# Re-weighting and interleaving the background feed of an FFT-convolution plus feed-forward kernel

## The chip, the cores and the metric

The kernel runs on one core of one Trainium2 chip. TensorE (PE) does the matmuls, VectorE (DVE) and ScalarE (ACT) the elementwise work, GpSimd (POOL) some elementwise work and one DMA queue, SyncE (SP) the other DMA queue. The metric is the device time of one execution in microseconds; a time is given as the median of its runs.

## The reference

Two stages are computed, in fp32. The first is a long convolution: `u = x * v` is convolved along the sequence (12480 positions, 4 batches, 128 channels) with a filter that a small network makes from position embeddings, and the result is multiplied by `x`. The second sends all 49920 tokens through a gated feed-forward layer of width 2048.

```python
h_filt = (np.maximum(pos_emb @ w1, 0.0) @ w2) * np.exp(-0.01 * pos)[:, None]
Uf = np.fft.rfft(x * v, n=2 * S, axis=1)
Hf = np.fft.rfft(h_filt, n=2 * S, axis=0)
y = np.fft.irfft(Uf * Hf[None, :, :], n=2 * S, axis=1)[:, :S, :]
a = (x * y).reshape(B * S, D)
h = a @ w_in
out = (h * (1.0 / (1.0 + np.exp(-1.702 * h)))) @ w_out
```

## The kernel before

**The work.** The sequence is cut in two blocks and the four batches are taken in parts, which gives five sets, numbered 0 to 4 (`SETS`). For each set the convolution has three phases. First transforms (`p1_unit`, 26 a set) multiply `x` and `v`, fold the product, split it in two parts (`uh` on ACT at L295, `ul` on DVE at L298) and do a first Fourier stage on PE (L178 to L180), storing to DRAM `g_d`. Spectral units (`p2_unit`, 31 a set) load `g_d`, do the second stage forward on PE (L324), multiply spectra on DVE, do the inverse on PE (L330, copied out at L473) and store `z_d`. Output units (`p3_unit`, 104 in all) load `z_d` on POOL's queue (L499), do the last inverse stage on PE (L520) and multiply by `x`, which gives the input tiles `xh` and `xl` of the feed-forward layer.

**Set 3 and 4 differ from 1 and 2 in their spectral units.** They belong to the second block and also add the product of the older spectrum: on DVE two products at L419 or L423, the products with the forward's result at L438 and L439, the adds at L441 and L443, and the final subtract and add that give `y` at L463 and L464. A spectral unit of set 1 or 2 has its products at L459 and L461 instead.

**The feed-forward steps.** `Ffn.mm1` (L592 to L594) and `Ffn.mm2` (L609) run 832 times, eight for each output unit; one such pair is called a step here, t = 0 to 831. A step's matmuls of the second layer come three steps behind those of the first. Between them DVE makes `fgl` (L600) from two ACT results, `fgh` and `fg`; `fg` has two buffers.

**The order.** It is written out by hand. Set 0's first two phases run ahead of the steps. From step `HOLD` on, each step gives sets 1 to 4 a share of the background work by `feed.run(1.0)`; at every eighth step an output unit of the current set is started (`p3.tick`). At step `HOLD` a pool is closed, its memory taken over and the padding of `z_d` filled with zeros. The output units of sets 1 to 4 begin at steps 95, 199, 407 and 615; a set's spectral units have to be done by then, and `feed.reach` gives out what is left.

**The planner.** `conv_feed` lists the units in order, each with a weight, and a mark (the sum of weights) for the end of each set's spectral units. `Feed.pace` sets the rate so that a mark is reached in a given number of steps. Starting a unit lets every unit that is still in `Pipe` go on to its next `yield` (a tick); a `yield 1` within a tick ends an atom only. `Feed.run` gives out the n-th atom of a tick when the goal passes `base + w * n / size`, where `size` is the number of atoms of the tick before; atoms beyond that number fall due at `base + w`. Units of `None` start nothing and only move the pipe on. A first transform takes seven ticks (loads, constants, small network, product and fold, `ul`, matmuls, store), a spectral unit of set 3 or 4 six (loads, nothing, forward with all DVE work, nothing, inverse registered, store). The inverse of a unit is issued ahead of the next unit's forward (`behind`) or at its own last tick.

**Buffers that matter.** `ft`, the constants of a first transform, has four buffers and is loaded on POOL's queue (L278); the lone pair at the end of a set takes two. The PSUM tag `cv` has three banks, of which a forward takes two.

Of the kernel before, what the change touches and what calls it, by code (L numbers as in the profile page):

```python
# [28 lines left out]
NP = N2 // 2  # L29
LONE = NP - 1  # L30
NV = (KZ // 2 + 1) // 2
# [4 lines left out]
STEPS = FC // 2  # L36
KEEP = 24
AHEAD = 2
HOLD = 14
WHEN = (1, 5, 9, 13, 17, 21, 24, 28)  # L40

PAIRS = [(n, N2 - n) for n in range(1, NP)] + [(0, NP)]
# [73 lines left out]
def conv_ffn_kernel(  # L116
# [114 lines left out]
    def p1_start(p):  # L231
        c, h = divmod(p, 2)
        if h == 0 and c + AHEAD < NP // 2:
            p1_load(c + AHEAD)
        x2, fl, pt = shared["in", c]
        yield
        if h == 0:
            shared["rt"] = mlp_in(pt, "p1")
        rt = shared["rt"]
        yield  # L240
        u = sb("u", [M, 2, 2, 128], F32, 2)
        nc.gpsimd.tensor_tensor(out=u[:, :, 1], in0=x2[:, h, 0], in1=x2[:, h, 1], op=ALU.mult)
        mlp_out(u, rt, 0, p)
        yield
        if p == LONE:
            pq = u
        else:
            pq = sb("pq", [M, 2, 2, 128], F32, 2)
            fold(pq, u)
        yield  # L250
        t, bs = pair(True)
        for ri in range(2):
            if p == LONE:
                for q in range(2):
                    mm(out=bs[ri][:, q * 256:(q + 1) * 256], lhsT=fl[h + ri][:, q],
                       rhs=pq[:, ri].rearrange("p b c -> p (b c)"), start=True, stop=True)
            else:
                mm(out=bs[ri], lhsT=fl[h][:, ri], rhs=flat(pq), start=True, stop=True)
        a = sb("a", [KP, 2, 512], F32, 3)
        act(a, t, ACTF.Copy)  # L260
        yield
        yield
        g_out(0, p, a)
# [116 lines left out]
    def spec_store(eu, w0, nw, q=nc.sync):  # L380
        q.dma_start(out=e_d[0][:, w0:w0 + nw], in_=eu[:, 0, 0:nw])
        q.dma_start(out=us_d[0][:, 0, w0:w0 + nw], in_=eu[:, 1, 0:nw])
# [239 lines left out]

    def conv_feed():
        p1 = {j: [(p1_unit(j, p), 1.6 if j == 1 else 1.4) for p in range(NP)] for j in range(1, 5)}
        ahead = {2: 5, 3: 16, 4: 16}
        units, marks = list(p1[1]), []
        for j in range(1, 5):
            nxt = p1.get(j + 1, [])
            n = ahead.get(j + 1, 0)
            units += nxt[:n]  # L630
            units += [(p2_unit(j, v), 2.4) for v in range(NV)]
            m = 8 if j == 1 else NP - n
            units += nxt[n:n + m]
            if j >= 3:
                units += [(None, 2.0)] * 12
            marks.append(sum(w for _, w in units))
            units += nxt[n + m:]
        return units, marks

    def fill(o, q):  # L640
        d = z_d[o][:, KZ:KP].rearrange("r k (q c) -> r (k q) c", c=128)
        q.dma_start(out=d, in_=zero.unsqueeze(1).broadcast_to([128, d.shape[1], 128]))

    with tc.manual_schedule():
        keep_cm = tc.tile_pool(name="keep", bufs=1, side="right", reuse_waits="tile")
        with tc.tile_pool(name="ps0", bufs=3, space=PSUM) as ps0, tc.tile_pool(name="ps0b", bufs=1, space=PSUM) as ps0b, \
# [26 lines left out]
            units = [p1_start(p) for p in range(NP)] + [None] * 5  # L673
# [19 lines left out]
        def when(n):  # L693
            return (n - 1) * STEPS - 1

        first = {next(i for i, hv in enumerate(HV) if hv[0] == o): o for o in range(1, 5)}
        begin = sorted(when(n) for n in first)
        feed = Feed(pipe, *conv_feed())
        feed.pace(0, begin[0] - HOLD)
        for n in range(7):  # L700
            p3.tick(p3_unit(n // 6) if n in (0, 6) else None)
            if n == 1:
# [8 lines left out]
        for n in range(NH):  # L711
            for k in range(STEPS):
                if pend:
                    ffn.lo(pend[-1])
                if len(pend) == LAG - 1 and pend[0][1] == STEPS - 1:
                    ffn.mm2(pend.pop(0))
                pend.append(ffn.mm1(n, k))
                t = n * STEPS + k
                if t == 1:
                    nc.gpsimd.tensor_tensor(out=sgn0, in0=gate[:, 0:1], in1=gate[:, 0:1], op=ALU.mult)  # L720
                if t == 1 or t == 9:
                    for _ in range(KEEP // 2):
                        spec_store(*spectra.pop(0), nc.gpsimd)
                if t == HOLD:
                    keep_cm.__exit__(None, None, None)
                    for o in range(1, 5):
                        fill(o, nc.gpsimd)
                    ps["s"] = ctx.enter_context(tc.tile_pool(name="main", bufs=1, side="right", reuse_waits="tile"))
                if len(pend) == LAG:
                    ffn.mm2(pend.pop(0))  # L730
                if t >= HOLD:
                    feed.run(1.0)
                new = None
                if k == STEPS - 1 and n + 2 < NH:
                    if n + 2 in first:
                        o = first[n + 2]
                        feed.reach()
                        if o < 4:
                            feed.pace(o, begin[o] - begin[o - 1] - 2)
                        else:  # L740
                            feed.rate = 0.0
                    new = p3_unit(n + 2)
                p3.tick(new)
                if k == 4:
                    ffn.store()
# [127 lines left out]
```

## Time and profile before

| | us |
|---|---|
| median of 3 runs | 3045.15 |
| lowest and highest | 3041.74, 3048.4 |
| profiled execution | 3039.97 |
| its span | 3038.2 |

| engine | busy, us | share of the span |
|---|---|---|
| PE | 2978.5 | 98% |
| DVE | 2145.6 | 71% |
| ACT | 2091.7 | 69% |
| POOL | 464.9 | 15% |

PE is busy nearly all the time, so the share alone does not tell much: what can be won is what little it idles, and what its clock loses. The stages differ. Set 0 fills the first 200 us; the steps begin at 202.9 us; sets 1 to 4 are fed beside them up to about 2300 us; the rest is steps and output units alone. The windows view of the profile, which gives busy time and granted clock for stretches of the span, is read stage by stage below.

### The profile page before, as it was taken

Reading aid. Unit: us, or ns where it says so; the run is one execution under the profiler, and the core shown is the slowest. Engines: PE = TensorE matmul, PEld = TensorE weight load, DVE = VectorE, ACT = ScalarE, POOL = GpSimd, SP = SyncE. Lnnn points to the kernel's source line nnn. Section 1 sums busy time; section 2 is a strip of 40 time slices with the busy share of each in tenths; the row PEclk is TensorE's granted clock in tenths of the full one; section 3 lists DMA queues with packets and bytes.
Section 4 is the critical chain, followed back from the end, with each engine's and each line's share of the span. In section 5 each row is a group of like instructions: output and inputs, shape, how many; then the busy total and the mean of one; then the engine's idle time right before and its main releaser. Section 6 shows DMA issues by size and latency. Waiting matters only on the chain.

```text
span 3038.2 us, 42541 instructions
## 1 busy us (share of the span) xinstructions
PE 2978.5 (98%) x15508; PEld 2349.1 (77%) x15508; DVE 2145.6 (71%) x2909; ACT 2091.7 (69%) x2689; POOL 464.9 (15%) x765
## 2 busy tenths in 40 slices
PE   8999999999999999999999999999999999999999
PEld 4467876688666788777778877777778888888887
DVE  7645677877778667999996469898895444444444
ACT  3466776788777677666667766666667677776776
POOL 1353110022011121110111111111111111111110
PEclk9999999999999899999999999999999999999999
DMA  9889899999778876655655325455541111111110
GB/s 295 291 281 285 241 291 286 291 327 308 247 265 279 247 207 195 206 179 192 204 182 164 119 86 166 148 178 159 168 143 63 62 46 46 61 46 46 61 46 27
DMA packets 261104, 541.87 MB, mean 178 GB/s; under 512 B 30978, under 2 KB 120762, under 8 KB 260898
## 3 DMA queue, kind: packets, MB, share of 16 engines
q1 hardware_dynamic: 205970, 377.29, 39.0%
q0 software_dynamic: 54928, 161.86, 17.8%
q8 instruction: 125, 2.05, 0.3%
q14 instruction: 81, 0.66, 0.1%
HBM read 330.24 MB, written 208.80 MB: 177 GB/s over the span
## 4 chain that ended last, share of the span: by engine, by line
issue 41%; PE 13%; DVE 7%; POOL 5%; DMA 1%; ACT 0%; POOLq 0%; SPq 0%; DVEq 0%
PE h L592 5%; PE acc L609 5%; DVE fgl L600 2%; POOL zt L499 2%; DVE t L423 2%; POOL out_dram L620 1%; POOL vt L495 1%; PE cv L520 1%; POOL x L497 1%; DVE t L438 1%; DVE t L439 1%; DVE t L443 1%; PE cv L178 1%; PE cv L179 1%; PE cv L180 1%
## 5 line engine op out<-in xcount | busy, mean ns | idle before, releaser
L600 DVE TENSOR_TENSOR fgl<-fg,fgh 128x960 fp32r<-128x960 f32 x832 | 956.3, 1153 | 427.7 <-ACT fg L594 425.0
L593 ACT ACTIVATE fgh<-h 128x960 fp32r<-128x960 f32 x832 | 809.8, 973 | 536.6 <-PE h L592 536.0
L592 PE MATMUL h<-xh,wi 128*128 128x480 f32 x3328 | 1148.1, 386 | 12.5 <-ACT fg L594 11.9
L609 PE MATMUL acc<-fgh,wo 128*128 128x480 f32 x3328 | 866.8, 382 | 0.0
L594 ACT ACTIVATE fg<-h 128x960 f32<-128x960 f32 x832 | 804.2, 967 | 65.6 <-DVE fgl L600 65.2
L592 PEld LDWEIGHTS h<-xh,wi 128*128 128x128 f32 x3328 | 627.2, 188 | 187.8 <-ACT fg L594 37.8
L609 PEld LDWEIGHTS acc<-fgh,wo 128*128 128x128 f32 x3328 | 625.6, 188 | 110.8 <-issue 12.9
L592 PE MATMUL h<-xl,wi 128*128 128x480 f32 x1664 | 633.6, 381 | 2.0 <-DVE xl L541 2.0
L609 PE MATMUL acc<-fgl,wo 128*128 128x480 f32 x1664 | 502.6, 383 | 5.2 <-DVE fgl L600 5.2
L620 POOL DMA_DIRECT2D out_dram<-ot x104 | 58.2, 559 | 1966.9 <-ACT ot L613 1909.9
L609 PEld LDWEIGHTS acc<-fgl,wo 128*128 128x128 f32 x1664 | 312.8, 188 | 57.5 <-DVE fgl L600 7.8
L592 PEld LDWEIGHTS h<-xl,wi 128*128 128x128 f32 x1664 | 313.4, 188 | 50.2 <-DVE xl L541 5.0
L520 PEld LDWEIGHTS cv<-vt,zt 122*128 122x128 f32 x1664 | 203.3, 194 | 25.8 <-issue 15.0
L520 PE MATMUL cv<-vt,zt 122*128 122x120 f32 x1664 | 208.2, 278 | 5.2 <-issue 3.6
L530 DVE TENSOR_TENSOR a<-cv,yq 128x240 f32<-128x240 f32 (+1 forms) x101 | 40.6, 402 | 208.9 <-ACT yq L528 208.9
L324 PE MATMUL cv<-g,wf 52*64 52x512 f32 (+1 forms) x1240 | 178.9, 589 | 7.5 <-DMA g<-g_d 7.2
L499 POOL DMA_DIRECT2D zt<-z_d x204 | 148.0, 733 | 8.5 <-issue 6.5
L311 ACT ACTIVATE a<-cv 128x512 f32<-128x512 f32 x208 | 120.5, 600 | 19.8 <-PE cv L180 11.2
L473 ACT ACTIVATE z<-ab 128x1024 f32<-128x1024 f32 (+2 forms) x124 | 112.5, 908 | 27.9 <-PE ab L330 25.2
L278 POOL DMA_DIRECT2D ft<-in_c_f_dram x108 | 58.0, 539 | 445.4 <-PE cv L180 430.6
L330 PE MATMUL ab<-t,wv 52*64 52x512 f32 (+2 forms) x992 | 120.4, 555 | 1.2 <-ACT fg L594 1.2
L459 DVE TENSOR_TENSOR t<-us,e 128x512 f32<-128x512 f32 (+2 forms) x62 | 58.5, 943 | 85.1 <-PE ab L330 51.2
(90 smaller groups left out, 2552.6 us busy)
## 6 DMA issues: line engine op xcount, KB each, us to landing
g_d<-a SPq DMA_DIRECT2D x260, 256.0 KB
g<-g_d SPq DMA_DIRECT2D x300, 208.0 KB
zt<-z_d POOLq DMA_DIRECT2D x204, 256.0 KB, 5.5
e<-e_d SPq DMA_DIRECT2D x180, 256.0 KB
z_d<-z SPq DMA_DIRECT2D x90, 512.0 KB
xt<-in_xv_dram SPq DMA_DIRECT2D x78, 480.0 KB
u<-us_d SPq DMA_DIRECT2D x60, 512.0 KB
ft<-in_c_f_dram POOLq DMA_DIRECT2D x108, 240.0 KB, 4.9
```

The costliest lines, as they stand in the source:

```text
L311: act(a[:, ri], b, ACTF.Copy)
L324: mm(out=xy[q ^ c][64 * c:64 * c + 64, 0:256 * nw].rearrange("p (w c) -> p w c", w=nw), lhsT=wf[64 * q:64 * q + N2, c], rhs=g[64 * q:64 * ...
L330: mm(out=ab[h][64 * pl:64 * pl + 64, 0:w].rearrange("p (w c) -> p w c", w=nw), lhsT=wv[64 * h:64 * h + N2, pl], rhs=y[pl ^ h][64 * h:64 * ...
L473: act(zv.rearrange("p w a c -> p a w c"), ab[:, :, 0:wd].rearrange("p a (w c) -> p a w c", w=nw), ACTF.Copy)
L499: q.dma_start(out=zv[:, gq], in_=z_d[o][64 * gq + 2 * p0:64 * gq + 2 * p0 + 2 * npr].rearrange("r k c -> k r c"))
L520: mm(out=b[:, c0:c0 + M], lhsT=lhs, rhs=rhs, start=(k == 0), stop=(k == 1))
L592: mm(out=h[:, i, 0:TW], lhsT=wt[:, s], rhs=xx, start=st, stop=sp)
L593: act(gh, h[:, :, 0:TW], ACTF.Gelu_apprx_sigmoid)
L594: act(gf, h[:, :, 0:TW], ACTF.Gelu_apprx_sigmoid)
L600: tt(out=gl, in0=gf, in1=gh.bitcast(F32), op=ALU.subtract)
L609: mm(out=acc, lhsT=wt[:, 2 * k + i, :], rhs=xx[:, i], start=(t == 0 and i == 0 and k == 0), stop=(t == 2 and i == 1 and k == STEPS - 1))
L620: nc.gpsimd.dma_start(out=out[:, n], in_=ot)
```

## The change

It touches the planner alone; no instruction is added or taken away.

- `HOLD` goes from 14 to 16: pool change, zero fill and feeding start two steps later.
- The spectral units of sets 3 and 4 weigh 4.0 instead of 2.4.
- Set 4's first transforms: before, 16 stand ahead of set 3's spectral units and 10 behind. After, 8 stand ahead and the other 18 alternate with spectral units of set 3, one behind each of the first 18; the last 13 spectral units stand alone.
- The twelve empty units at the end of sets 3 and 4 weigh 0.5 each instead of 2.0.
- The first pace aims six steps ahead of `begin[0] - HOLD` (73 steps instead of 81), the others six steps ahead of the next begin instead of two.

```diff
-HOLD = 14
+HOLD = 16
...
-        ahead = {2: 5, 3: 16, 4: 16}
+        ahead = {2: (5, 8), 3: (16, 10)}
         units, marks = list(p1[1]), []
         for j in range(1, 5):
-            nxt = p1.get(j + 1, [])
-            n = ahead.get(j + 1, 0)
-            units += nxt[:n]
-            units += [(p2_unit(j, v), 2.4) for v in range(NV)]
-            m = 8 if j == 1 else NP - n
-            units += nxt[n:n + m]
-            if j >= 3:
-                units += [(None, 2.0)] * 12
+            p2 = [(p2_unit(j, v), 2.4 if j < 3 else 4.0) for v in range(NV)]
+            if j < 3:
+                nxt = p1[j + 1]
+                n, m = ahead[j + 1]
+                units += nxt[:n] + p2 + nxt[n:n + m]
+            else:
+                side = p1[4] if j == 3 else []
+                units += side[:8]
+                for v in range(NV):
+                    units += [p2[v]] + side[8 + v:9 + v]
+                units += [(None, 0.5)] * 12
             marks.append(sum(w for _, w in units))
-            units += nxt[n + m:]
+            if j < 3:
+                units += nxt[n + m:]
...
-        feed.pace(0, begin[0] - HOLD)
+        feed.pace(0, begin[0] - HOLD - 6)
...
-                            feed.pace(o, begin[o] - begin[o - 1] - 2)
+                            feed.pace(o, begin[o] - begin[o - 1] - 6)
```

## The prediction

> **What bounds the kernel now.** I read the page first, then stretches of the span cut at the starts of feed-forward steps, then groups and time line inside the stretches that lose time. In the fence: the page's TensorE row and two slice rows, then the windows view (length, busy time and count by engine, granted clock, DMA share, GB/s).
>
> ```profile
> PE 2978.5 (98%) x15508; PEld 2349.1 (77%) x15508; DVE 2145.6 (71%) x2909; ACT 2091.7 (69%) x2689; POOL 464.9 (15%) x765
> DVE  7645677877778667999996469898895444444444
> PEclk9999999999999899999999999999999999999999
> ...
> 245.80:287.30 41.50, 37.40 (x170) 31.52 (x169) 24.62 (x48) 26.76 (x42) 7.99 (x14) 0.96 0.94 257
> 406.00:576.90 170.90, 168.64 (x999) 114.11 (x998) 127.91 (x226) 114.98 (x179) 17.78 (x29) 1.00 0.92 285
> 576.90:742.80 165.90, 165.45 (x822) 137.98 (x821) 129.01 (x216) 136.46 (x204) 33.91 (x59) 1.00 1.06 316
> 964.90:1006.60 41.70, 36.17 (x191) 23.58 (x190) 32.52 (x43) 26.66 (x37) 4.81 (x8) 0.91 0.83 280
> 1041.00:1076.30 35.30, 31.68 (x144) 27.21 (x143) 17.86 (x26) 22.85 (x32) 8.34 (x14) 0.90 0.76 204
> 1185.30:1583.60 398.30, 386.69 (x2064) 292.46 (x2063) 397.58 (x540) 256.50 (x301) 44.90 (x74) 1.00 0.61 194
> 1834.40:2277.10 442.70, 442.70 (x2338) 348.99 (x2337) 399.88 (x474) 300.77 (x351) 51.77 (x85) 1.00 0.50 161
> 2417.30:3008.90 591.60, 591.60 (x2913) 515.71 (x2912) 286.17 (x311) 417.32 (x493) 76.68 (x126) 1.00 0.15 50
> ```
>
> TensorE (PE) is the bound almost everywhere, so moving its work gains nothing by itself; gains and losses are the times when it waits. Counting idle time plus (1 - clock) x busy as lost, today's holes are: the start of the transforms (245.8) 4.1 + 1.5 = 5.6 us; the end of set 2 (964.9) 5.5 + 3.3 = 8.8; the first output unit of set 2 (1041.0) 3.6 + 3.2 = 6.8; and set 3's spectral units (1185.3), where VectorE is busy 397.58 of 398.30. Set 4's stretch (1834.4) and the plain tail (2417.3) have no hole.
>
> How much set 3's stretch loses follows from three groups (instructions, count | busy, mean); the first line is of the tail, the next two of set 4's stretch, the last three of set 3's.
>
> ```profile
> L593 ACT ACTIVATE fgh<-h 128x960 fp32r<-128x960 f32 x208 | 202.6, 974 | 153.4 <-PE h L592 153.4
> ...
> L593 ACT ACTIVATE fgh<-h 128x960 fp32r<-128x960 f32 x137 | 133.4, 974 | 109.3 <-PE h L592 109.3
> L473 ACT ACTIVATE z<-ab 128x1024 f32<-128x1024 f32 x27 | 27.7, 1025 | 11.7 <-PE ab L330 11.7
> ...
> L593 ACT ACTIVATE fgh<-h 128x960 fp32r<-128x960 f32 x113 | 109.8, 972 | 66.0 <-PE h L592 66.0
> L324 PE MATMUL cv<-g,wf 52*64 52x512 f32 (+1 forms) x248 | 31.9, 584 | 0.0
> L473 ACT ACTIVATE z<-ab 128x1024 f32<-128x1024 f32 x29 | 29.8, 1029 | 2.0 <-PE ab L330 2.0
> ```
>
> One L593 is one step; the windows open on one, and close on one that the counts 137 and 113 include. A plain step is 591.6 / 208 = 2.844 us. A spectral unit of set 4 adds (442.7 - 136 x 2.844) / 27 = 2.07 us of PE. Set 3's stretch has 112 steps, 30 units (248 / 8 = 31 forwards, 29 inverses) and two first-transform units of some 1.4 us: 318.5 + 62.1 + 2.8 = 383.4, so **14.9 us** are lost there to VectorE (DVE). By the same division DVE needs 286.17 / 208 = 1.376 us a step and (397.58 - 112 x 1.376) / 30 = 8.1 us a unit, first transforms included.
>
> **The plan, before and after.** `Feed` gives out positions; marks and rates follow from the diff. Before: marks 134.2, 263.2, 398.0, 496.4, rates 1.657, 1.248, 0.642, 0.471 a step. After: marks 134.2, 263.2, 429.6, 559.6; the rates are 134.2/73 = 1.838, (263.2 - 147.1)/98 = 1.185, (429.6 - 270.3)/202 = 0.789, (559.6 - 434.3)/202 = 0.620 (the goal runs on past each mark to the next set's begin).
>
> **Set 3, its average (gain).** A spectral unit now comes every 4.0/0.789 = 5.07 steps (before 2.4/0.642 = 3.74). The 13 that stand alone at the end need 5.07 x 1.376 + 8.1 = 15.1 us of DVE in 5.07 x 2.844 + 2.07 = 16.5 us of PE: 91%, and set 4 today has 399.88/442.70 = 90% with no hole. The 14.9 us go: **-15** (-15 to -8). Set 4's own wider spacing (6.45 steps for 5.09) gains nothing, since PE already has no hole there.
>
> **Set 3, the alternation (loss).** This is the step that decides. `run` spaces a unit's atoms by `size`, the atom count of the unit before. A tick started by a spectral unit has 13 atoms (older first transform's two matmul groups 2, registering an inverse 1, another's u/pq/uh 1, the spectral unit of age two 7, two loads); one started by a first transform has 5. So behind a 5 the first five of the 13 are spread over the weight of 4.0 and the other eight fall due together at its end, with the next tick's: second product of the old spectrum, forward, all products, adds, y, and then `ul` (L298) of a first transform, in one step. Its matmuls come 1.4/0.789 = 1.78 steps later. How long that chain is, the first set-4 unit of today shows (time line: start, length, engine, line):
>
> ```profile
> 1795.04 1.09 PE L324 MATMUL cv<-g,wf 52*64 52x512 f32 x8
> 1796.05 0.48 PE L592 MATMUL h<-xh,wi 128*128 128x480 f32 x1
> 1796.19 0.69 DVE L438 TENSOR_TENSOR t<-cv,e 128x512 f32<-128x512 f32 x1 [1.96 <-PE cv L324]
> ...
> 1801.49 1.09 PE L324 MATMUL cv<-g,wf 52*64 52x512 f32 x8
> 1801.59 0.69 DVE L464 TENSOR_TENSOR t<-t,t 128x512 f32<-128x512 f32 x1
> ...
> 1814.10 0.70 PE L609 MATMUL acc<-fgl,wo 128*128 128x480 f32 x2 [1.71 <-DVE fgl L600]
> 1815.94 1.94 PE L520 MATMUL cv<-vt,zt 122*128 122x120 f32 x16
> ...
> L298 DVE TENSOR_TENSOR ul<-pq,uh 120x512 fp32r<-120x512 f32 x100 | 68.5, 685 | 16.1 <-ACT uh L295 15.8
> L423 DVE TENSOR_TENSOR t<-u,e 128x512 f32<-128x512 f32 (+1 forms) x124 | 76.9, 673 | 0.0
> L419 DVE TENSOR_TENSOR t<-u,e 128x1024 f32<-128x1024 f32 (+1 forms) x62 | 73.3, 1200 | 0.0
> L530 DVE TENSOR_TENSOR a<-cv,yq 128x240 f32<-128x240 f32 (+1 forms) x101 | 40.6, 402 | 208.9 <-ACT yq L528 208.9
> ```
>
> From the forward's end (1796.1) DVE needs until 1802.3 for products to y, and with `ul` behind it until 1802.9. PE does two steps of feed-forward matmuls by 1801.5 and needs `ul` at its second transform matmul, 0.2 us later: a wait of **1.2 us**. Laying the positions out, 17 units have their `ul` behind such a chain, v = 0 to 16, up to step 326: in 13 the matmuls are two steps off (13 x 1.2 = 15.6), in four one step off (2.7 us less cover): steps 258 and 306 have an output unit's 1.9 us between (2.0 each), 265 has none (3.9), 217 is half spread (1.2). Sum **+25**. Queued behind `ul` on DVE is `fgl` of that step, which PE needs only a step later. Bounds: 0, if the chain hides; and 16 times a half-speed stretch of 3.4 us more (1.7 lost each), +52; I take the waits alone, since the 1.71 us wait above is the nearest row, and the clock was 1.00 right behind it:
>
> ```profile
> 1811.20:1814.60 3.40, 1.69 (x8) 1.16 (x7) 3.40 (x5) 1.90 (x3) 0.00 (x0) 1.00 0.93 313
> 1814.60:1818.00 3.40, 3.40 (x25) 3.17 (x25) 3.40 (x5) 2.78 (x5) 2.19 (x4) 1.00 0.56 176
> ...
> 988.50:991.90 3.40, 3.40 (x10) 2.78 (x10) 2.57 (x4) 2.27 (x5) 0.00 (x0) 0.50 1.02 338
> 1002.20:1009.00 6.80, 5.26 (x16) 3.96 (x20) 5.17 (x10) 4.76 (x6) 0.00 (x0) 0.50 0.48 149
> ```
>
> The Trainium skill (TensorE: Matmul & The Clock Gate, section Part 1: The HAM clock gate) says that the clock halves after an idle window of some 3.4 us. By that rule the waits stay at 25, by a gate that trips at 1.3 us they would be 52. The first two rows bear the rule out; the rows at 988.5 and 1002.2, behind the gaps shown below of 1.31 and 3.84 us, are half-speed, so the trace trips at less than the rule says.
>
> **The drains (loss).** Empty units now weigh 0.5: a tick every 0.63 step behind set 3, 0.81 behind set 4. The last two spectral units do all their DVE work in steps 394 and 395, and both last inverses stand in step 396 in front of PE's next matmuls. From the forward of unit 29 DVE has 6.1 + 0.8 (L530, L531) + 1.15 (L600) + 4 x 0.673 + 6.1 = 16.9 us; PE has 1.9 + 5.4 + three transforms of 1.05 = 10.5: a wait of 6.4 us, and about 2 at half clock: **+8.5** (3 to 13). Set 4 (steps 600 to 603): DVE 6.1 + 1.15 + 2.4 + 6.1 = 15.8 against PE 8.2 + 3.2 + 1.9 = 13.3; with clock and the two `fg` buffers **+5** (0 to 10). Today these drains are spread: behind set 4 at 4.2 steps a tick, with no hole.
>
> **The end of set 2 (gain).** Time line around both holes:
>
> ```profile
> 987.06 1.01 PE L324 MATMUL cv<-g,wf 52*64 52x256 f32 x8 [1.31 <-DMA g<-g_d]
> 996.19 0.69 DVE L459 TENSOR_TENSOR t<-us,e 128x512 f32<-128x512 f32 x1 [5.08 <-ACT fg L594]
> 1001.34 0.63 ACT L295 ACTIVATE uh<-pq 120x512 fp32r<-120x512 f32 x1 [4.18 <-DVE pq L189]
> 1003.74 0.77 PE L592 MATMUL h<-xh,wi 128*128 128x480 f32 x1 [3.84 <-ACT fg L594]
> ...
> 1035.91 0.52 POOL L278 DMA_DIRECT2D ft<-in_c_f_dram  x1 [3.48 <-PE cv L180]
> 1047.06 1.43 POOL L499 DMA_DIRECT2D zt<-z_d  x2 [1.52 <-DMA xt<-in_xv_dram]
> 1053.86 4.04 PE L520 MATMUL cv<-vt,zt 122*128 122x120 f32 x16 [3.62 <-issue]
> ```
>
> The last spectral unit starts at step 184 today, 179 after. Its forward then follows its load by three steps, not two, and the `uh` that blocks ACT comes a step behind the inverse that frees DVE, not in the same one. At 1047.06 the loads of output unit 26 (issued at step 199) are late because POOL's queue waits with `ft` for PE, the lone pair holding two of four `ft` buffers from step 198 to 205; after, it holds them from 194 to 198. I take 15 of the 16.6 us with its neighbour at 1006.6 (1.0): **-15** (-18 to -4).
>
> **Sets 1 and the start.** Feeding starts two steps later, with the zero fill, and `zt` of unit 3 goes ahead of the fill: **-2** of 5.6 (-5.6 to +3). Set 1 is fed 1.838/1.657 = 11% denser: 285 GB/s would become 316, which 576.9 carries with 0.5 us of idle; PE's idle there, 2.3 us, may double or treble, and by step 95 some eight first transforms more are through: **+4** (-2 to 23, eight steps of 2.844, if transfers bound it). They are missing later, at no gain, PE being full there.
>
> **Sum:** -15 + 25 + 8.5 + 5 - 15 - 2 + 4 = **+10.5 us** on the profiled execution, 3039.97 us (span 3038.2 and 1.8 around it). That one lies 5.2 us under the median of 3045.15; on the median the sum gives 3055.7, and I write **3056**.
>
> **Rivals.** (1) The alternation's chain hides (DVE starts earlier, or PE is late for another reason), and the gains stay: 0 for 25, so -14.5: 3031. For it: DVE's average is only (6.85 x 1.376 + 8.1 + 2.2)/(6.85 x 2.844 + 3.5) = 86%. It decides where the chain from forward to `ul` falls under 5.6 us. Faster. (2) Half of the waits hide, where output units or a late PE lie between: 10.5 - 12.5 = -2, 3043: no change. (3) Each wait trips the clock: +27 more, 3083; the row at 1814.6 speaks against it. (4) Set 1 becomes bound by transfers, +19 more: 3075. (5) The aim of six steps does nothing at step 199, because POOL's queue and not the late z_d holds the loads, and set 2's hole stays: +11 more, 3067.
>
> **Chances.** Forecast 0.36, (1) 0.19, (2) 0.21, (3) 0.05, (4) 0.09, (5) 0.10. What can be told from no change here is about 0.2%, 6 us: faster 0.19, same 0.21, slower 0.60. The range reaches from between (1) and (2) to (4): 3033 to 3077.
>
> **What would show it.** Right: between steps 223 and 333 PE idle before L179 put down to `ul`, 1 to 2 us each, DVE busy in bursts with idle between; two PE gaps before L330 at steps 396 and 603; no gap at 1041; set 3's last stretch with DVE near 90%. Wrong: PE without idle through the alternation, or inverses at the drains without a wait; or a hole grown in the first 600 us.

## The result and the profile after

The changed kernel is slower: **3082.72 us** against 3046.78 us before (medians of four runs each), a ratio of 1.0126 with an interval of 1.0113 to 1.0139. The prediction was 3056 us with a range up to 3077: the direction was right, the size was not, and the time lies outside the range. The profiled execution took 3081.62 us, its span 3079.9 us, 41.7 us more than the profiled span before. Both profiled executions are at the low end of their runs; between the medians the rise is 35.9 us.

The page of the changed kernel, its rows for busy time and for VectorE's 40 slices:

```profile
PE 2996.4 (97%) x15508; PEld 2352.4 (76%) x15508; DVE 2150.8 (70%) x2909; ACT 2087.4 (68%) x2689; POOL 464.8 (15%) x765
...
DVE  7646677676777777777789858888888644454444
```

As many instructions as before; PE's busy time grew by 17.9 us, so the rest of the 41.7 is idle. DVE's slices 21 to 31, 96469898895 before, read 89858888888 now: they are more even, as the new weights meant them to be. None of this says where the time went. For that the span is cut at the same steps in both kernels. First the windows view of the kernel before (length, busy time and count of PE, PEld, DVE, ACT, POOL, then clock, DMA share, GB/s) for steps 48 to 95, 104 to 111 and 216 to 351:

```profile
406.00:611.90 205.90, 203.49 (x1197) 140.86 (x1196) 159.28 (x283) 142.80 (x224) 22.36 (x38) 1.00 0.93 286
644.80:677.20 32.40, 32.40 (x155) 27.69 (x154) 25.34 (x43) 27.34 (x41) 4.73 (x9) 1.00 1.07 321
1103.90:1583.60 479.70, 468.09 (x2457) 362.66 (x2456) 448.00 (x612) 320.06 (x386) 58.52 (x97) 1.00 0.63 196
```

The same view of the changed kernel: steps 0 to 23, 48 to 95, 104 to 111, 176 to 215, 216 to 351, 352 to 391, 392 to 407, 600 to 615:

```profile
203.00:280.00 77.00, 76.02 (x369) 65.20 (x368) 45.65 (x67) 56.93 (x76) 39.55 (x70) 1.00 0.97 313
407.60:646.60 239.00, 224.30 (x1232) 152.07 (x1232) 171.99 (x307) 152.54 (x244) 26.85 (x46) 0.96 0.90 282
677.60:715.90 38.30, 34.66 (x162) 29.55 (x161) 24.99 (x41) 27.57 (x41) 7.95 (x14) 0.96 0.90 267
966.70:1122.10 155.40, 152.29 (x767) 120.93 (x766) 112.02 (x163) 118.92 (x163) 26.23 (x45) 0.99 0.91 276
1122.10:1612.50 490.40, 464.69 (x2353) 369.61 (x2352) 387.50 (x519) 323.27 (x401) 62.11 (x103) 0.99 0.56 166
1612.50:1742.80 130.30, 130.30 (x689) 102.64 (x688) 119.49 (x157) 88.49 (x103) 15.22 (x25) 1.00 0.53 170
1742.80:1800.90 58.10, 54.11 (x273) 43.09 (x273) 39.14 (x53) 35.40 (x41) 6.10 (x10) 0.94 0.47 150
2406.40:2458.70 52.30, 51.27 (x274) 40.79 (x272) 34.85 (x44) 35.40 (x42) 6.10 (x10) 1.00 0.24 82
```

Two stretches carry the loss. In steps 48 to 95, set 1's spectral units, PE idles 14.7 us and the clock takes .04 x 224 = 9 us, where before it idled 2.4 us at full clock. In steps 216 to 351, the alternation, it idles 25.7 us where it idled 11.6. A stretch does not hold the same background work in both kernels, so lengths alone mislead. The table therefore takes from each stretch the PE work in it: every matmul at the price that it has where nothing waits (0.218 us for a feed-forward matmul and 0.114 for one of L520, which give the plain step of 2.844 us; the background's likewise by their columns). What is left is time lost. A wrong price stands alike in every column (other prices for the background's matmuls shift set 1's row by some 3 us, all columns together), so the differences are what to read. The experiments' columns belong to the sections that follow.

| us lost in steps | before | after | x1 | x3 | x4 | x6 | x8 | x13 |
|---|---|---|---|---|---|---|---|---|
| 0-23, start | 6.7 | 1.4 | 1.4 | 1.4 | 1.4 | 1.4 | 1.5 | 1.4 |
| 24-95, set 1 | 14.4 | 43.1 | 17.4 | 18.0 | 40.8 | 38.3 | 8.5 | 10.1 |
| 96-111 | 0.3 | 5.6 | -0.2 | 5.0 | 5.2 | 7.9 | 0.3 | -0.2 |
| 112-175 | 2.9 | 1.9 | 10.2 | 1.9 | 1.8 | 2.0 | 9.1 | 3.9 |
| 176-215, end of set 2 | 18.2 | 6.5 | 4.1 | 6.7 | 2.5 | 4.4 | 4.4 | 4.9 |
| 216-351, alternation | 13.5 | 33.5 | 35.3 | 33.4 | 1.6 | 42.9 | 6.0 | 5.9 |
| 392-431, drain of set 3 | 3.1 | 8.5 | 8.2 | 8.5 | 8.2 | 3.9 | 4.2 | 4.1 |
| 600-615, drain of set 4 | 0.0 | 1.4 | 1.3 | 1.3 | 2.5 | 0.4 | 0.7 | 0.6 |

From before to after: -5.3, +28.7, +5.3, -1.0, -11.7, +20.0, +5.4, +1.4 are +42.8, and the steps not listed give -1; the span grew by 41.7. In x6, x10 and after, which do the same in their first 95 steps, set 1 lost 38.3, 43.2 and 43.1: a few us there are scatter.

The waits view of PE in the alternation, after (who waited for whom, us in total, times, longest):

```profile
PE cv L179 <- DVE ul L298: 23.3, 17, 3.8
PE h L592 <- DVE xl L541: 1.7, 1, 1.7
```

Seventeen waits for `ul` of 23.3 us were found where the prediction laid out 17 of 25 us. The time line has their three kinds (start, length, instruction, idle before it and who ended it):

```profile
1257.24 0.50 PE L179 MATMUL cv<-ul,ft 120*128 120x512 f32 x1 [1.14 <-DVE ul L298]
1280.42 0.51 PE L179 MATMUL cv<-ul,ft 120*128 120x512 f32 x1 [2.00 <-DVE ul L298]
1306.23 0.50 PE L179 MATMUL cv<-ul,ft 120*128 120x512 f32 x1 [3.75 <-DVE ul L298]
...
1765.09 1.37 PE L330 MATMUL ab<-t,wv 52*64 52x256 f32 x8 [3.99 <-DVE t L463]
```

Thirteen are of 1.14 us, where the matmuls come two steps behind the chain; two are of 2.00, where an output unit lies between at one step; one is of 3.75, where nothing does; the first, at step 218, is of 0.81. Predicted were 1.2, 2.0, 3.9 and 1.2. The last line is the drain of set 3, a single inverse that waits for DVE. What the prediction had far too small is the hole in set 1.

### The profile page after: what moved, and what is told of

It reads as the page before. It is cut to its first block, busy times and chain, and to the rows that moved or that the text cites. A ratio compares the mean times of both kernels' runs of the same rounds, so it can differ in the third digit from the quotient of the medians.

```text
span 3079.9 us, 42578 instructions
## 1 busy us (share of the span) xinstructions
PE 2996.4 (97%) x15508; PEld 2352.4 (76%) x15508; DVE 2150.8 (70%) x2909; ACT 2087.4 (68%) x2689; POOL 464.8 (15%) x765
## 4 chain that ended last, share of the span: by engine, by line
issue 57%; PE 26%; POOL 7%; DMA 4%; DVE 4%; ACT 1%; SPq 0%; POOLq 0%; ACTq 0%; DVEq 0%
PE h L592 8%; PE acc L609 8%; PE cv L324 3%; POOL zt L499 2%; DMA g<-g_d 2%; POOL vt L495 1%; POOL out_dram L620 1%; PE cv L520 1%; POOL x L497 1%; PE wb L670 1%; PE ab L330 1%; PE cv L178 1%; PE cv L179 1%; PE cv L180 1%; DMA g_d<-a 1%
## 5 line engine op out<-in xcount | busy, mean ns | idle before, releaser
L592 PE MATMUL h<-xh,wi 128*128 128x480 f32 x3328 | 1151.0, 387 | 3.7 <-ACT fg L594 3.3
L592 PEld LDWEIGHTS h<-xh,wi 128*128 128x128 f32 x3328 | 629.3, 189 | 181.9 <-issue 59.1
L592 PE MATMUL h<-xl,wi 128*128 128x480 f32 x1664 | 634.4, 381 | 2.6 <-DVE xl L541 2.6
L592 PEld LDWEIGHTS h<-xl,wi 128*128 128x128 f32 x1664 | 314.6, 189 | 49.2 <-DVE xl L541 3.8
L520 PEld LDWEIGHTS cv<-vt,zt 122*128 122x128 f32 x1664 | 202.5, 193 | 25.2 <-issue 14.9
L520 PE MATMUL cv<-vt,zt 122*128 122x120 f32 x1664 | 206.7, 278 | 5.0 <-DMA zt<-z_d 4.4
L324 PE MATMUL cv<-g,wf 52*64 52x512 f32 (+1 forms) x1240 | 185.1, 594 | 13.7 <-DMA g<-g_d 11.5
L438 DVE TENSOR_TENSOR t<-cv,e 128x512 f32<-128x512 f32 (+1 forms) x124 | 84.0, 678 | 84.3 <-PE cv L324 84.3
L473 ACT ACTIVATE z<-ab 128x1024 f32<-128x1024 f32 (+2 forms) x124 | 112.4, 907 | 40.8 <-PE ab L330 34.3
L311 ACT ACTIVATE a<-cv 128x512 f32<-128x512 f32 x208 | 120.0, 602 | 25.2 <-PE cv L180 16.1
```

The source lines that it names most:

```text
L311: act(a[:, ri], b, ACTF.Copy)
L324: mm(out=xy[q ^ c][64 * c:64 * c + 64, 0:256 * nw].rearrange("p (w c) -> p w c", w=nw), lhsT=wf[64 * q:64 * q + N2, c], rhs=g[64 * q:64 * ...
L473: act(zv.rearrange("p w a c -> p a w c"), ab[:, :, 0:wd].rearrange("p a (w c) -> p a w c", w=nw), ACTF.Copy)
L520: mm(out=b[:, c0:c0 + M], lhsT=lhs, rhs=rhs, start=(k == 0), stop=(k == 1))
L592: mm(out=h[:, i, 0:TW], lhsT=wt[:, s], rhs=xx, start=st, stop=sp)
```

## The experiments

Every kernel here computes the whole of the reference. Lines of the edited kernels are shifted by up to four. Ratios are against the kernel before on the same chip.

### Which part of the change makes the hole in set 1

**x1** is the changed kernel with the first pace back.

```diff
-        feed.pace(0, begin[0] - HOLD - 6)
+        feed.pace(0, begin[0] - HOLD)
```

> The changed kernel with the first pace alone put back (134.2/79 = 1.699 a step, not 1.838). Theory (set 1 fed denser is what went wrong): the hole of steps 24 to 95, 43 us in the changed kernel against 14 before, shrinks to some 17, and with it the time by 25 to 31 us, to about 3055. Rival (the hole comes from the later start or from what follows it): 3078 to 3085, as the changed kernel.

Measured: 3062.01 us, ratio 1.0056 (1.0041 to 1.0071). Set 1 loses 17.4 us instead of 43.1, as good as before, and the hole at steps 104 to 111 is gone. In its place 7.5 us are lost in steps 112 to 135, at the next output unit, which is why the time fell by less than expected. So the first pace, which feeds set 1 in 73 steps instead of 79 here (81 in the kernel before), costs some 26 us in set 1.

**x2** is the kernel before with that part alone, so that nothing of sets 3 and 4 is changed.

```diff
-HOLD = 14
+HOLD = 16
...
-        feed.pace(0, begin[0] - HOLD)
+        feed.pace(0, begin[0] - HOLD - 6)
```

> The kernel before with only the later start (HOLD 16) and the six-step aim of the first pace. Theory: the hole of set 1 appears without the rest of the change: +20 to +35 us on the kernel before, 3065 to 3082. Rival (it needs the rest): 3040 to 3050.

Measured: 3054.66 us, ratio 1.0031 (1.0017 to 1.0044), less than expected. The hole is there in full: set 1 loses 46.3 us against 14.4. What the expectation left out is that the shift also repairs other places: the start loses 1.4 for 6.7, and the end of set 2 loses 5.7 for 18.2. x1, with the old first pace and the new later ones, loses 4.1 there: either shift of the plan takes most of the hole at the end of set 2 away (both kernels also have the later start).

### Why set 1 loses: transfers, or the order in a queue

The prediction's rival was that set 1 becomes bound by transfers. The other theory: the loads of `g` are issued late, because they stand in SP's queue behind transfers that wait for DVE. **x3** sends the same bytes, with set 1's `g` loads on POOL's queue.

```diff
+        dq = nc.gpsimd if j == 1 else nc.sync
         for q in range(2):
             r = slice(64 * q, 64 * q + N2)
-            nc.sync.dma_start(out=g[r, 0:nw].rearrange("p w a c -> p (w a) c"), in_=g_d[j][r, 4 * v:4 * v + 2 * nw])
+            dq.dma_start(out=g[r, 0:nw].rearrange("p w a c -> p (w a) c"), in_=g_d[j][r, 4 * v:4 * v + 2 * nw])
```

> The changed kernel with the loads of g of set 1's spectral units issued on POOL's queue instead of SP's; bytes and order of the work stay. Theory (in SP's queue these loads stand behind stores that wait for DVE and so are issued too late): PE's waits for g between steps 48 and 88, 6.6 us with their half clock behind them, nearly go, and the time falls by 12 to 25 us, to 3058 to 3070. Rival (the transfers' bandwidth is used up): no change, 3078 to 3085. Second rival (DVE's waits for inverses set the stage): g's waits go, but the time moves by less than 6 us.

Measured: 3059.53 us, ratio 1.005 (1.0035 to 1.0065). Steps 48 to 95 lose 10.0 us instead of 35.2; before they lost 10.9. Its windows row for these steps, and its row of DMA issues for `g` (KB each, median us from issue to landing):

```profile
409.00:622.80 213.80, 206.82 (x1232) 147.87 (x1231) 171.89 (x307) 152.08 (x244) 51.65 (x94) 0.99 0.96 313
```

```profile
g<-g_d POOLq DMA_DIRECT2D x46, 208.0 KB, 5.7
```

The same PE matmuls (1232) and the same transfers now take 213.8 us instead of 239.0, at 313 GB/s instead of 282. Transfers were not the bound. A load of `g` lands 5.7 us after its issue here, on POOL's queue; for SP's queue the view gives no landing. The waits of PE for it are gone; before, after and in x3 (407.6 to 646.6 after, the same steps in the others), the waits view of PE has:

```profile
PE cv L324 <- DMA g<-g_d: 2.1, 2, 1.8
```

```profile
PE cv L324 <- DMA g<-g_d: 6.6, 7, 2.1
PE cv L178 <- ACT a L311: 4.3, 2, 4.1
```

```profile
PE cv L178 <- ACT a L311: 4.2, 2, 4.0
```

The waits alone are small. Of the 25.2 us that x3 wins, 7.7 are idle and 17.5 are PE's busy time, 224.30 to 206.82 for the same matmuls. The clock (0.96 to 0.99) gives some 7 of these. Much of the rest are waits too, which the trace counts as busy time: the eight matmuls of a forward mostly start within 0.45 us, but when the last six wait, the first two are recorded as running for 1.04 us meanwhile. Over set 1's 31 forwards the starts spread 18.0 us beyond that 0.45 after, of which 4.9 are recorded as idle; the spread was 7.9 before and is 1.4 in x3.

The time line of SP in the changed kernel shows what stands ahead of the loads (lengths are those of the issue):

```profile
524.15 0.34 SPq L392 DMA_DIRECT2D e<-e_d  x1
524.55 0.42 SPq L480 DMA_DIRECT2D z_d<-z  x1
526.67 0.32 SPq L454 DMA_DIRECT2D e_d<-e  x1
527.09 0.41 SPq L455 DMA_DIRECT2D us_d<-us  x1
527.59 1.69 SPq L337 DMA_DIRECT2D g<-g_d  x2
```

From the time lines of DVE and of PE there:

```profile
525.78 0.87 DVE L452 SCALAR_TENSOR_TENSOR e<-e,sgn_sb,cv 128x256 f32<-128x256 f32 x2
```

```profile
533.83 1.04 PE L324 MATMUL cv<-g,wf 52*64 52x512 f32 x2 [0.75 <-DVE t L459]
536.99 1.98 PE L324 MATMUL cv<-g,wf 52*64 52x512 f32 x6 [2.12 <-DMA g<-g_d]
538.90 0.77 PE L592 MATMUL h<-xh,wi 128*128 128x480 f32 x1
```

The store at L454 needs DVE's L452 of the unit that went forward at 522.58. It is issued at 526.67 when that has ended, and only then come the two loads, issued by 529.28. They are the loads of the unit that goes forward at 533.83, whose last six matmuls wait until 536.99. So the next load hangs on a store that hangs on a forward: a loop through SP's queue. The table has the lead of set 1's loads (from the end of a pair's issue to the start of its forward, 31 pairs in each trace) and the mean time from one forward to the next:

| | lead, median | lower quartile | from forward to forward |
|---|---|---|---|
| before | 5.6 us | 5.0 us | 6.05 us |
| after | 6.4 us | 4.1 us | 6.36 us |
| x3 | 23.4 us | 21.8 us | 5.50 us |

With the 5.7 us that a load takes in x3, the kernel before had already no margin. Fed 11% denser, its units did not come faster but slower, every 6.36 us, with ten of them torn (over 1.4 us from the first to the last forward matmul) where three were before. The median lead did not fall, but its lower quartile did. With the loads out of the queue they come every 5.50 us.

Which transfer holds SP up? Waits view of SP, before (406.0 to 611.9) and after (407.6 to 604.1):

```profile
SPq L392 <- DVE t L461: 50.6, 25, 6.6
SPq L454 <- DVE e L452: 35.7, 29, 4.8
```

```profile
SPq L392 <- DVE t L461: 43.4, 23, 6.0
SPq L454 <- DVE e L452: 32.5, 27, 2.7
```

The load of `e0` waits for a buffer that L461 still reads, the stores wait for L452. SP stood there no less before: its waits are not new, the denser feed beside them is. **x9** moves the first, **x11** the others, **x12** both to POOL's queue.

```diff
-        nc.sync.dma_start(out=e0[:, 0:nw], in_=e_d[0][:, w0:w0 + nw])
+        (nc.gpsimd if j == 1 else nc.sync).dma_start(out=e0[:, 0:nw], in_=e_d[0][:, w0:w0 + nw])
```

> The changed kernel with only the load of e0 (L392) of set 1's spectral units on POOL's queue; g and the stores stay on SP's. Theory (SP's queue stands at e0, whose two buffers wait for DVE's second product L461 of the unit two before, and g of the next unit is behind it): the hole of steps 48 to 95 falls from 35 us under 18 and the time by 12 to 22 us, to 3060 to 3071. Rival (the stores of e and us, L454 and L455, hold the queue as much): the hole stays over 28 us and the time over 3074.

```diff
-                nc.sync.dma_start(out=e_d[1][:, w0:w0 + nw], in_=e1[:, 0:nw])
-                nc.sync.dma_start(out=us_d[0][:, 1, w0:w0 + nw], in_=us[:, 0:nw])
+                nc.gpsimd.dma_start(out=e_d[1][:, w0:w0 + nw], in_=e1[:, 0:nw])
+                nc.gpsimd.dma_start(out=us_d[0][:, 1, w0:w0 + nw], in_=us[:, 0:nw])
```

> The changed kernel with only the two stores of e and us (L454, L455) of set 1 on POOL's queue; g and e0 stay on SP's. Theory, mended by the run with e0 alone (there SP's waits moved to the stores, 98 us at L454, and the hole stayed): the stores are what g stands behind, so the hole of steps 48 to 95 falls from 35 under 20 us and the time to 3062 to 3073. Rival (either of the two is enough to hold the queue): the hole stays over 28 us, the time over 3074, and SP's waits are at e0, L392.

The kernel of the last of the three has both edits.

> The changed kernel with both e0 and the stores of e and us of set 1 on POOL's queue, g on SP's. Theory (SP's queue in step with DVE makes g late): with nothing of DVE ahead of g, the hole of steps 48 to 95 falls near that of g on POOL's queue, 10 us, and the time to 3056 to 3066. Rival (putting g on another queue helped for another reason than the order in SP's): hole over 25 us.

| | us | ratio | lost in steps 48-95 |
|---|---|---|---|
| x9, `e0` | 3088.11 | 1.0141 (1.012 to 1.0162) | 33.6 |
| x11, stores | 3072.46 | 1.0098 (1.0083 to 1.0113) | 20.1 |
| x12, both | 3066.74 | 1.0076 (1.0061 to 1.0091) | 19.9 |

The waits view of SP in each (x9, x11, x12), its largest row:

```profile
SPq L454 <- DVE e L452: 98.4, 29, 10.0
```

```profile
SPq L392 <- DVE t L461: 103.3, 28, 10.3
```

```profile
SPq L480 <- ACT z L473: 102.8, 24, 10.6
```

The idea that one transfer, `e0`, is at fault fell with x9: the wait moves to the next one in line. Whichever is taken out, SP stands some 100 us at another, up to the stores of z that wait for ACT. Taking the stores out, alone or with `e0`, wins 15 of the 35 us; taking the loads out wins 25. How long SP stands says little; the lead tells more: its median is 6.3 us in x9, 7.2 in x11 and 13.6 in x12, and 7, 2 and 1 of the 31 forwards are torn.

Neither theory nor rival of x12 foresaw 19.9 us. The waits view of PE in it, steps 48 to 95, largest rows, shows why x12 is no better than x11:

```profile
PE cv L520 <- DMA zt<-z_d: 7.5, 6, 3.5
PE cv L178 <- DMA ft<-in_c_f_dram: 2.4, 1, 2.4
```

PE waits for `g` no more, though its loads are still on SP's queue; so it was the order in that queue and not the queue itself that made them late. What PE waits for now are loads on POOL's queue, which has taken over the transfers that stand for DVE. How much of the 19.9 us these waits cost was not tried.

### The hole at steps 104 to 111

After, the time line has at this place, on POOL and on PE:

```profile
676.61 0.52 POOL L278 DMA_DIRECT2D ft<-in_c_f_dram  x1 [6.11 <-PE cv L180]
680.62 0.52 POOL L278 DMA_DIRECT2D ft<-in_c_f_dram  x1 [3.48 <-PE cv L180]
...
682.22 1.53 POOL L499 DMA_DIRECT2D zt<-z_d  x2
```

```profile
691.46 0.68 PE L520 MATMUL cv<-vt,zt 122*128 122x120 f32 x4 [3.11 <-DMA zt<-z_d]
```

It is what the prediction described for step 199 before: `ft` loads wait in POOL's queue for PE to free a buffer, and the loads of the next output unit, issued at last at 682.22, stand behind them. Then, it was at output unit 26; now the lone pair at the end of set 2's first transforms meets unit 14. **x10** takes that unit's loads out of the queue.

```diff
-        q = nc.gpsimd if n > 1 else nc.sync
+        q = nc.gpsimd if n > 1 and n != 14 else nc.sync
```

> The changed kernel with the loads of output unit 14 alone (issued at step 103) on SP's queue. Theory (in POOL's queue they stand behind ft loads that wait for PE while the lone pair of set 2 holds two of the four buffers): the hole of steps 104 to 111, 5.7 us, falls under 1.5, and the time by 3 to 6 us, to 3077 to 3080, if the rest keeps. Rival (z_d of set 1 or the transfers themselves are late): the hole stays over 4 us.

Measured: 3079.89 us, ratio 1.0114 (1.0099 to 1.0129). The stretch 104 to 111 loses 0.0 us instead of 5.7, and no wait of PE is left in it. (In x10 these `zt` loads go out at 675.25, ahead of the `ft` load that is there at 678.16.) The time of the whole differs from the changed kernel's by less than the two intervals allow to tell (1.0099 to 1.0129 against 1.0113 to 1.0139), so the cause of the hole is shown by its stretch, its price only there.

### The alternation

**x4** spaces a tick's atoms by the number that the last tick of the same weight had, instead of the tick before.

```diff
         self.size = 6
+        self.sizes = {}
...
+                self.size = self.sizes.get(self.w, self.size)
...
-                    self.size = max(self.n, 1)
+                    self.size = self.sizes[self.w] = max(self.n, 1)
```

> The changed kernel with the atom count remembered for each weight, so that a tick is spaced by the count of the last tick of its own kind. Theory of the burst (set 3's alternation): the waits of PE's L179 for ul, 23.3 us in 17 waits, fall under 3 us, and the time by 20 to 26 us, to about 3059. Rival (those waits come from the alternation itself, two kinds of unit sharing DVE): the waits stay over 12 us and the time over 3070.

Measured: 3047.65 us, ratio 1.0013 (1.0003 to 1.0022), a larger gain than expected. Windows row of the alternation, and the largest wait of PE in it (here L181 and L300 are the L179 and L298 of the kernel before):

```profile
1113.70:1572.20 458.50, 457.03 (x2352) 368.22 (x2351) 384.89 (x519) 324.53 (x401) 62.10 (x103) 1.00 0.60 178
```

```profile
PE cv L181 <- DVE ul L300: 0.8, 1, 0.8
```

As many matmuls on PE within one of 2353, as many instructions on DVE (519), and 458.5 us instead of 490.4: 31.9 us less, 24.2 of it idle and 7.7 in PE's busy time. Waits for `ul` fall from 23.3 to 0.8 us. This is the clearest answer of the study: neither the new weights nor the alternation costs much by itself (1.6 us are lost there in x4); the spacing by the wrong tick's atom count does. The expectation counted waits and a little clock. It missed that the matmul behind a wait also takes longer: it is recorded with 0.50 us, where in a row of matmuls each adds 0.23. Over the stretch the L179 matmuls add 13.8 us to PE's busy time after and 9.5 in x4, which is 4.3 of the 7.7; two stretches at half clock, which cost 1.7 each, are the rest.

### The drains

**x6** lets the empty units weigh three times as much, but seven of them.

```diff
-                units += [(None, 0.5)] * 12
+                units += [(None, 1.5)] * 7
```

> The changed kernel with seven empty units of weight 1.5 behind sets 3 and 4 in place of twelve of 0.5. Theory (two spectral units' DVE work in two steps, and the last inverse ahead of PE's next matmuls): the holes of steps 392 to 407 and 600 to 615, 7.1 and 1.4 us, fall under 1 each, and the time by 6 to 9 us, to 3074 to 3077; the waits for ul in the alternation stay. Rival (the holes belong to the end of a set, however it is spaced): 3080 to 3085.

Measured: 3085.71 us, ratio 1.0129 (1.0105 to 1.0153): no gain. The drains themselves are repaired: steps 392 to 407 lose 0.4 us instead of 7.1, 600 to 615 lose 0.4 for 1.4. But the weight of 10.5 in place of 6 raises the rate of set 3, and the alternation loses 42.9 us instead of 33.5. The waits of PE and the windows of 3.4 us behind one of its long waits, x6:

```profile
PE cv L179 <- DVE ul L298: 25.3, 13, 3.8
```

```profile
1371.00:1374.40 3.40, 2.20 (x5) 1.82 (x6) 3.40 (x5) 0.94 (x2) 0.00 (x0) 0.60 1.01 280
1374.40:1377.80 3.40, 3.40 (x10) 2.82 (x9) 1.02 (x2) 1.98 (x3) 0.00 (x0) 0.50 0.24 89
```

Thirteen waits instead of seventeen, but more of them of the one-step kind, and half clock behind those. The expectation held for the drains and not for the whole: the waits for `ul`, which were to stay, grew by 2 us and brought more half clock.

### Together

**x8** is the changed kernel with the edits of x1, x3, x4 and x6. **x13** adds output unit 15's loads on SP, since x8 still lost 6.4 us in steps 112 to 135, where the lone pair now meets that unit.

> The changed kernel with all four repairs together: first pace back, ticks spaced by the count of their own kind, drains of seven at 1.5, g of set 1 on POOL's queue. If the holes add as in the ledger of the runs so far: start 1.4, steps 24 to 47 2.6, steps 48 to 95 at most 8, the output unit near the lone pair 0 to 7.5, end of set 2 2.5, set 3 2, entry of set 4 1.4, together 18 to 26 us against 59 before: 3005 to 3016, faster than both kernels. Rival (the repairs take from each other, or a new wait takes over): over 3025.

Measured: 3018.51 us, ratio 0.9911 (0.9896 to 0.9926), a hair over the expectation.

```diff
-        q = nc.gpsimd if n > 1 else nc.sync
+        q = nc.gpsimd if n > 1 and n != 15 else nc.sync
```

> All four repairs together, and the loads of output unit 15 (issued at step 111, the hole of 5.6 us that is left there) on SP's queue. Theory: that hole goes, and the time falls by 4 to 6 us under that of the four repairs (3018.5), to 3012 to 3015. Rival: the hole moves to another unit, 3017 to 3021.

Measured: 3012.39 us (3007.23 to 3016.3), ratio **0.9894** (0.9877 to 0.991). It is faster than both kernels. Its windows of steps 48 to 95 and 216 to 351:

```profile
398.90:603.80 204.90, 200.34 (x1211) 140.79 (x1211) 161.43 (x288) 144.65 (x228) 51.91 (x96) 1.00 0.93 298
1087.00:1550.20 463.20, 459.23 (x2357) 369.18 (x2357) 389.71 (x526) 325.00 (x401) 62.13 (x103) 1.00 0.60 181
```

Both at full clock, with 4.6 and 4.0 us of idle. By the table, x13 is ahead of the kernel before by 13.3 us at the end of set 2, 7.6 in steps 216 to 351, 5.3 at the start and 4.3 in set 1. So the wider spectral units of set 3 are worth some 8 us here (11.9 in x4), less 1.6 at the drains; most of the gain comes from the shifted plan and from the loads moved to other queues. The repairs were not tried on the kernel before, so what each is worth without the change is not shown.

## Why the prediction was right and wrong

**The step that failed** is "Sets 1 and the start", its term for a denser set 1: +4 with bounds of -2 and 23. It came out at +28.7, beyond the upper bound; x1 gives 25.7 of it to the first pace, and x3 25.2 to where the loads of `g` are issued. The term was priced by transfers: 285 GB/s would become 316, and the stretch at 576.9 carried that. Two things were wrong in it. The stretch at 576.9 holds 16 forward matmuls of spectral units, the one at 406.0 held 224; it shows what the transfers carry where hardly a spectral unit runs. And the limit was none of bytes: in x3 the same bytes went through at 313 GB/s without the hole. It was the time from one spectral unit to the next through SP's queue, which the kernel before met with no margin (5.6 us of lead, where a load takes 5.7 in x3). The trace of before showed the sign: 2.1 us of PE waiting for `g` in set 1, and 86 us of SP waiting for DVE. The prediction's rival (4) named the right stage with the wrong cause, and its bound fell short for that.

**A moved hole.** +5.3 us at steps 104 to 111 were not in the sum. The prediction followed the lone pair of `ft` buffers only at step 199, where it was seen, and not where set 1's pace moves the first lone pair to. Its mechanism was right.

**The alternation.** Predicted +25 as 17 waits; measured 17 waits, 23.3 us, of the predicted lengths and within a step of the four places that were named. By x4 the price is 31.9 us: the mechanism and the waits were right, the term was too small. The 31.9 us are 22.5 of these waits, 4.3 of longer matmuls behind them, 3.4 of clock, and the wait of 1.7 for `xl` (L592), which is gone in x4 as well. Rivals (1) and (2), that the waits hide, fell: not one of the seventeen hides. Rival (3), that each wait trips the clock, fell as well: two did.

**Set 3's average.** -15 predicted; 13.5 lost before, 1.6 in x4: -11.9, in the bounds. The last stretch, steps 352 to 391, has DVE at 119.49 of 130.30 us, 92%, and PE without idle; the prediction had 91%.

**The end of set 2** came out at -11.7 for -15, **the start** at -5.3 for -2, both in their bounds. Rival (5), that step 199 keeps its hole, fell. **The drains**: +7.1 for +8.5 behind set 3. The wait that was foretold came, but of 3.99 us instead of 6.4, and the clock took some 3.4 us (0.94 over 58.1 us) instead of about 2; that the sum of the two is near is in part luck. It was +1.4 for +5 behind set 4, where no such wait came.

The sum had seven terms. Six were within their bounds and together 5 us too low, of which smaller gains elsewhere (steps 112 to 175, 352 to 391, 408 to 431) gave back 4. Set 1 and the moved hole make the rest: 24.7 + 5.3 = 30 of the 31 us between +10.5 and the span's +41.7.

**Left open:** steps 24 to 47 lose 7.9 us after and 8.0 in x3, for 3.5 before and 2.6 in x1. It comes with the first pace, and the loads of `g` are not its cause; what is was not tried. Nor was the wait of L178 for `a`, 4.3 us at the end of set 1, which x3 leaves as it was.

## What to carry to other kernels

A loop that runs through an in-order queue (load, compute, store, next load) has a latency of its own; feeding it faster than that made it slower here, although the transfers had room (282 GB/s, where 313 went through in x3), so look at the lead from a load's issue to its use and compare it with how long a load takes. A background planner that spaces work by what the tick before held puts bursts in front of small instructions that the bound engine needs; key the spacing by the kind of tick. And when a pace is shifted, every place where two streams share a small pool of buffers moves with it: look for the old hole at a new step.

## What the runs showed of the hardware

The granted clock behind PE's waits was neither free nor always halved. In the changed kernel's alternation none of the 1.14 us waits was followed by less than full clock. The 3.75 us wait at 1306.23 was; windows of 3.4 us behind it, and behind one of two 2.0 us waits (1455.94; the other one, 1280.42, left the clock alone):

```profile
1305.70:1309.10 3.40, 2.87 (x16) 2.79 (x17) 1.54 (x2) 0.60 (x1) 0.00 (x0) 0.74 1.09 318
1309.10:1312.50 3.40, 3.40 (x15) 3.03 (x15) 2.15 (x4) 1.19 (x2) 0.00 (x0) 0.76 1.06 330
...
1455.30:1458.70 3.40, 2.75 (x10) 2.33 (x11) 3.40 (x6) 1.00 (x2) 0.00 (x0) 0.83 1.04 233
1458.70:1462.10 3.40, 3.40 (x12) 2.79 (x12) 1.68 (x2) 1.95 (x4) 0.00 (x0) 0.67 0.73 248
```

Each pair adds up to 1.7 us lost: one stretch of 3.4 us at half speed. In x6 all four `ul` waits of 3.75 to 3.78 us had half clock behind them, for 3.4 or 6.8 us. In set 1 of the changed kernel it came behind waits of 0.75 and 2.12 us with two matmuls between them (at 536.8):

```profile
533.40:536.80 3.40, 1.04 (x2) 0.19 (x2) 1.80 (x4) 0.34 (x1) 0.00 (x0) 0.87 1.11 272
536.80:540.20 3.40, 3.21 (x9) 1.48 (x10) 0.77 (x2) 0.66 (x2) 0.00 (x0) 0.50 1.00 364
```

The rule of the Trainium skill that the prediction weighed (TensorE: Matmul & The Clock Gate, section Part 1: The HAM clock gate), an idle window of some 3.4 us, fits the waits of 1.14 and of 3.75 us; the 2.0 us wait and the pair of short ones in set 1 halved the clock at less, and there the measurement decides. What tells these from the wait at 1280.42 stays open; that the sparse 52x64 transforms beside them count as idle was not tried.
